# A fused chunked attention and gated MLP on one core: new order entries for the first 430 operations

## The chip, the cores and the metric

One core of a Trainium2 chip. The metric is the device time of one execution in microseconds (us). The kernel before took 373.89 us in the median of 3 runs.

## The reference

Chunked attention over 4 batches, 8 heads and 768 tokens with 8 memory keys, and behind it a gated MLP whose gate is mixed along the tokens:

```python
for c in range(nc):                        # 24 chunks of 32 queries, 16 keys left, 8 right
    k_full = np.concatenate([mem_k, k_ctx], axis=2)
    scores = scale * np.matmul(q_c, k_full.transpose(0, 1, 3, 2))
    a = np.exp(scores - np.max(scores, axis=-1, keepdims=True))
    a = a / (np.sum(a, axis=-1, keepdims=True) + 1e-09)
    out[:, :, c_start:c_end] = np.matmul(a, v_full)
...
h = np.maximum(x @ w_in, 0.0)              # x: 4 x 768 x 512, w_in: 512 x 1024
u, v = (h[..., :d_ff // 2], h[..., d_ff // 2:])
v_n = (v - mu) / np.sqrt(var + 1e-06)
v_s = np.einsum('ts,bsd->btd', w_spatial, v_n) + b_spatial[None, :, None]
return ((u * v_s) @ w_out).astype(np.float32)
```

## The kernel before

The whole kernel is first written down as a list of operations in an object Plan (calls of `op`, numbered 0, 1, 2, ... in the order in which the program makes them) and then laid out by a planner, Plan.order, which runs through the operations with estimated durations, load times and semaphore delays and so makes five fixed lists, one for each of TensorE (PE), ScalarE (ACT), VectorE (DVE), GpSimd (POOL) and SyncE (SP). Each engine works its list strictly in that order and waits at an operation whose inputs aren't there. The planner takes, on each engine, the operation with the smallest sum of possible start and `wait`, and at equal sums the smaller `rank`; of the engines it then advances the one with the earliest pick. An operation that two engines could do stays with the one that would end it first, unless it is pinned. The table ORDER changes this by operation number: it adds to the rank, sets the wait (in us), and pins it to an engine:

```python
if n in ORDER:
    more, wait, only = ORDER[n]
    rank += more
    if only:
        eng = {only: eng[only]}
...
c = (late + ops[n][10], ops[n][4], n)
if pick is None or c < lead:
    pick, lead = (late, ops[n][4], n), c
...
if pick and (best is None or pick < best[0]):
    best = (pick, e)
```

A token tile is 128 tokens, a batch has six (blocks 0 to 5, 6 to 11, ...). For each block `attend` does the keys' rearrangement (`prep`), a burst of 64 small matmuls for the scores, row maximum, subtraction, exponential, row sum and reciprocal (`softmax`), a transposition of the probabilities (`pt`, `pT`), 64 small matmuls with v, the division (`xs`), and a second transposition into x (`xt`, then a high part on ScalarE, line 1122, and a low part on VectorE, line 1126). From block 4 on a burst joins a block's scores and the block before's product with v. Every large product is made of three matmuls (high by high, low by high, high by low), so x and all weights exist as a high and a low part. w_in arrives as 64-bit numbers in eight pieces of 512 KB (four rows of tiles by two halves) and each goes through `from_f64`: a scale (line 1733 or 1735), a shift and a sign step on VectorE (1743, 1749), the high part (597), the rest (1739), an add on GpSimd (1754) and the low part (1761). A v group (`ffn_v`) is 12 matmuls of 512 columns on one block's x with w_in's second half; a u group (`ffn_u`) is 12 matmuls of 384 columns on three blocks' x with a quarter of the first half. Both are line 1172.

The operations that the prediction speaks of, by number. 0, 2, 3: first small loads on ScalarE's queue. 4 to 9: six copies that spread the memory's v rows into the places of blocks 0 to 5 (`first_mem`, line 597). Each place is overwritten in part by that block's v loads, so these loads, on SyncE, wait for the copy. 10, 11 and on: loads, all on SyncE and chained one behind the other in the order of the constant FIRST. 14 to 20 and 22 to 28: the steps of w_in's pieces (1, second half) and (0, second half), 22 being the second one's scale. 56 to 62, 64 to 70, 75 to 81, 83 to 89: the pieces of the first half; 59 and 67 are two high parts, 83 the last piece's scale and 87 its rest step. 97 to 106: shift copies of v for blocks 1 to 5 (line 848). 109 on: blocks 0 to 6; 124 is block 1's exponential (line 1033), 158 block 3's reciprocal, 162 the high part of block 2's x. 207 to 273: the spatial weights, batch 1's v and w_out. 274 on: v and u groups of batch 0, then blocks 7 to 9. The base rank is 10 times the block's number, with 0.5 more for its x, 5 more for its shift copies; for the pieces of w_in it is the fourth field of their entry in FIRST (with 1 more for the rest, the add and the low part); entry 124 has 10, 99 and 100 have 25, 158 has 30.6, 162 has 30.5, 83 has 42.

A load waits until all but 2,000,000 bytes of the loads before it have landed, and for its buffer.

Of the kernel before, what the change touches and what calls it, by code (L numbers as in the profile page):

```python
# [45 lines left out]
    0: (117.6, 6, ''), 1: (1.7, 0, ''), 2: (0, 0.8, ''), 3: (4.8, 0, ''), 5: (20.5, 3, ''),  # L46
    6: (-8.1, 0.4, 'ACT'), 7: (49.4, 6, 'POOL'), 8: (7.1, 0, ''), 9: (-4.8, 0.2, 'ACT'), 10: (48.5, 0.8, ''),
    11: (0, 0.8, ''), 12: (20.6, 0, ''), 13: (-19.7, 0, ''), 14: (36, 0, ''), 15: (26.5, 0.8, ''),
    16: (12.7, 0.4, ''), 17: (16.5, 0, ''), 18: (9, 0.4, ''), 19: (5.9, 0, ''), 20: (10.7, 6, ''),
    21: (24.5, 0.8, ''), 22: (40.1, 3, 'POOL'), 23: (-4.6, 0, ''), 24: (-30.7, 0, ''), 25: (77.8, 0, ''),  # L50
    26: (-164.9, 3, ''), 28: (1.3, 0.8, ''), 29: (-34.6, 1.5, ''), 32: (0, 1.5, ''), 33: (-50.9, 0, ''),
    34: (-67.3, 6, ''), 35: (70.3, 0.2, ''), 36: (-13.8, 0, 'ACT'), 37: (54.9, 0, ''), 39: (21.1, 0, 'ACT'),
    41: (-5.5, 0, ''), 42: (-58.3, 0, 'DVE'), 43: (-7.9, 1.5, ''), 44: (-15.9, 1.5, ''), 45: (-4.8, 0, ''),
    46: (-35.8, 0.8, ''), 47: (0.9, 0, ''), 48: (-53.2, 0, ''), 49: (9.4, 1.5, ''), 50: (-22.6, 0.4, ''),
    51: (-1.6, 0, 'ACT'), 52: (-1.4, 0, ''), 53: (-174.4, 0, ''), 54: (10, 0, 'POOL'), 55: (3.7, 1.5, ''),
# [20 lines left out]
    162: (-45.5, 0, ''), 163: (16.9, 0, ''), 164: (13.1, 0, 'ACT'), 165: (60.6, 0, ''), 166: (-21.3, 0.8, ''),  # L76
# [1824 lines left out]
```

## Time and profile before

| what | value |
|---|---|
| median of 3 runs | 373.89 us (372.83 to 374.18) |
| the profiled execution | 373.35 us, its span 371.6 us |
| TensorE busy | 354.7 us, 95% of the span |
| ScalarE, VectorE, GpSimd busy | 266.4, 246.8, 164.4 us |
| moved | 42.08 MB, 113 GB/s in the mean |
| the chain that ended last | TensorE 89%, DMA 8%, ScalarE 1%, SyncE's queue 1% |

The table is an average over the span. In the page's 40 slices of 9.3 us TensorE is busy by three, seven, six tenths in the first three and by nine or more in all others to the last. The rows below are of the first stages. Times in them are counted from the first instruction; an idle time in brackets stands with the engine or transfer that ended it.

### The profile page before, as it was taken

What the parts mean: (1) busy time and instruction counts of PE and PEld (TensorE: products, weight loads), DVE (VectorE), ACT (ScalarE), POOL (GpSimd) and SP (SyncE); (2) the same over time, 40 slices, a digit from 0 to 9 for tenths busy, and PEclk for the clock granted to TensorE, in tenths of its full rate; (3) what the DMA queues carried; (4) which work ended last, traced back from release to release, by engine and by line L of the source; (5) the groups of instructions that cost most, each with busy time, mean ns of one, the idle gap of its engine ahead of it and who ended that gap; (6) DMA issues with size and microseconds to landing.
All of it is one profiled execution on the core that took longest, in us unless ns stands there. A gap on an engine that the chain in (4) does not pass through costs nothing.

```text
span 371.6 us, 11529 instructions
## 1 busy us (share of the span) xinstructions
PE 354.7 (95%) x4752; PEld 318.4 (86%) x4752; DVE 246.8 (66%) x497; ACT 266.4 (72%) x697; POOL 164.4 (44%) x249
## 2 busy tenths in 40 slices
PE   3769999999999999999999999999999999999996
PEld 3546797999899789899899889899899888999996
DVE  2878878877437375656537267575446798998694
ACT  6686899873585977977876968977966885664262
POOL 4764773573533341442634324424624743224632
PEclk9999999999999999999999999999999999999999
DMA  6989936782024253161024164142130140110004
GB/s 214 287 279 232 344 104 181 232 249 71 25 87 147 93 124 85 35 213 48 17 88 131 62 142 102 49 154 88 37 130 3 57 156 3 43 43 2 0 2 169
DMA packets 30828, 42.08 MB, mean 113 GB/s; under 512 B 5368, under 2 KB 24760, under 8 KB 30776
## 3 DMA queue, kind: packets, MB, share of 16 engines
q1 hardware_dynamic: 30552, 41.27, 36.4%
q8 instruction: 37, 0.61, 0.7%
q14 instruction: 15, 0.12, 0.1%
q10 hardware_dynamic: 224, 0.08, 0.1%
HBM read 35.05 MB, written 6.29 MB: 111 GB/s over the span
## 4 chain that ended last, share of the span: by engine, by line
PE 89%; DMA 8%; ACT 1%; SPq 1%; DVE 0%; issue 0%; ACTq 0%
PE f L1172 69%; PE sx L900 8%; PE f L1399 6%; DMA stage_w<-in_moe_w_in_dram 2%; PE f L1567 2%; DMA big<-in_moe_w_in_dram 2%; DMA q<-in_q_dram 2%; DMA k<-in_k_dram 1%; DMA v<-in_mem_v_dram 1%; SPq L623 1%; PE sx L1567 1%; PE xt L1567 1%; PE pt L1567 1%; PE xt L1116 1%; PE pt L1089 1%; ACT vmain L597 0%
## 5 line engine op out<-in xcount | busy, mean ns | idle before, releaser
L1172 PE MATMUL f<-x,win_h 128*128 128x384 f32 x256 | 72.4, 342 | 0.0
L1172 PE MATMUL f<-win_h,x 128*128 128x512 f32 x192 | 63.4, 411 | 0.5 <-ACT x L1122 0.3
L990 ACT COPY xs<-sx 32x128 f32<-32x128 f32 x240 | 61.6, 257 | 2.9
L1172 PE MATMUL f<-wout,big 128*128 128x512 f32 x216 | 55.7, 394 | 0.0
L1172 PEld LDWEIGHTS f<-x,win_h 128*128 128x128 f32 x256 | 47.0, 188 | 1.4
L1172 PEld LDWEIGHTS f<-wout,big 128*128 128x128 f32 x216 | 39.9, 188 | 7.0 <-DVE big L1671 0.2
L1172 PE MATMUL f<-x,win_l 128*128 128x384 f32 x128 | 43.3, 338 | 0.0
L1172 PEld LDWEIGHTS f<-win_h,x 128*128 128x128 f32 x192 | 35.4, 192 | 8.0 <-DVE x L1126 0.8
L1069 POOL TENSOR_TENSOR p<-p,rec 128x512 f32<-128x512 f32 x15 | 15.7, 1046 | 55.7 <-DVE rec L1046 54.8
L1664 POOL TENSOR_TENSOR st<-st,u 128x384 f32<-128x384 f32 x24 | 25.4, 1060 | 33.0 <-DVE st L1660 17.1
L597 ACT COPY pT<-p 32x128 f32<-32x128 f32 x128 | 37.9, 296 | 2.5 <-POOL p L1069 1.0
L1172 PE MATMUL f<-win_l,x 128*128 128x512 f32 x96 | 38.6, 402 | 0.0
L1218 POOL TENSOR_TENSOR rstd<-ve,mhalf 128x1 f32<-128x1 f32 x24 | 15.9, 663 | 49.5 <-DVE ve L1214 49.3
L597 POOL COPY pT<-p 32x128 f32<-32x128 f32 x112 | 35.5, 317 | 5.1
L1172 PE MATMUL f<-wsp_h,vb 128*128 128x384 f32 x144 | 37.3, 340 | 0.0
L1172 PE MATMUL f<-wsp_h,va 128*128 128x384 f32 x144 | 37.1, 339 | 0.0
L1660 DVE TENSOR_TENSOR st<-f,bias 128x384 f32<-128x384 f32 x24 | 13.4, 556 | 24.8 <-PE f L1172 24.6
L1033 ACT ACTIVATE p<-p 128x512 f32<-128x512 f32 x24 | 15.1, 629 | 19.1 <-DVE p L1018 16.2
L1172 PEld LDWEIGHTS f<-wsp_h,vb 128*128 128x128 f32 x144 | 26.0, 188 | 1.2
L1172 PEld LDWEIGHTS f<-wsp_h,va 128*128 128x128 f32 x144 | 26.0, 188 | 1.1
L900 PEld LDWEIGHTS sx<-k,q 64*32 64x32 f32 x1536 | 17.7, 112 | 9.7 <-issue 4.0
L1039 DVE TENSOR_REDUCE den<-p 128x8 f32<-128x512 f32 x24 | 16.4, 682 | 13.5 <-ACT p L1033 13.4
(225 smaller groups left out, 790.6 us busy)
## 6 DMA issues: line engine op xcount, KB each, us to landing
k<-in_k_dram SPq DMA_DIRECT2D x7, 800.0 KB
q<-in_q_dram SPq DMA_DIRECT2D x7, 768.0 KB
vmain<-in_v_dram SPq DMA_DIRECT2D x38, 128.0 KB
big<-in_moe_w_spatial_dram SPq DMA_DIRECT2D x12, 384.0 KB
out_dram<-st SPq DMA_DIRECT2D x18, 256.0 KB
vmain<-in_v_dram SPq DMA_DIRECT2D x37, 96.0 KB
big<-in_moe_w_in_dram SPq DMA_DIRECT2D x4, 512.0 KB
stage_w<-in_moe_w_in_dram SPq DMA_DIRECT2D x4, 512.0 KB
```

The lines of the kernel that those rows point to most:

```text
L597: return (nc.scalar.copy if e == "ACT" else nc.gpsimd.tensor_copy)(o, a).ins
L900: nc.tensor.matmul(o, w_, m, start=start, stop=True, skip_group_check=True)
L990: last_ = (nc.scalar.copy if e == "ACT" else nc.vector.tensor_copy)(o, a).ins
L1033: nc.scalar.activation(p3, p3, AF.Exp, scale=scale)
L1039: nc.vector.tensor_reduce(d, p3, axis=AX.X, op=ALU.add)
L1069: (nc.vector if e == "DVE" else nc.gpsimd).tensor_tensor(p3, p3, rec, op=ALU.mult)
L1172: return [nc.tensor.matmul(o, ll if x == 1 else lh, rl if x == 2 else rh, start=x == j == 0, stop=j == len(pairs) - 1 and x == (single[-1] ...
L1218: nc.gpsimd.tensor_tensor(a, t_["ve", i], mhalf, op=ALU.pow)
L1399: return [nc.tensor.matmul(o, l_ if x == 1 else h, w_[1] if x == 2 else w_[0], start=first and s == x == 0, stop=s == NQ - 1 and x == 2, s ...
L1567: return [nc.tensor.matmul(o, a[n == 1][:, cols], w2[n == 2], start=first and k == n == 0, stop=k == 1 and n == 2, skip_group_check=True). ...
L1660: nc.vector.tensor_tensor(alloc("st", s_, [P, HT], F32), t_["f", n], bias[:, tok], op=ALU.add)
L1664: nc.gpsimd.tensor_tensor(a, a, t_["u", i], op=ALU.mult)
```

## The change

All entries of ORDER for the operations 0 to 429 are replaced: other amounts added to the ranks (up to some thousands, where before they were up to 271), other waits, and other pins. Entries from 1236 on stay; operations 430 to 1235 have none, before and after. FIRST, the durations and everything else stay, so the loads keep their sequence on SyncE. Of the first 430 operations these lines of the diff hold the entries that the prediction names:

```diff
 ORDER = {
-    0: (117.6, 6, ''), 1: (1.7, 0, ''), 2: (0, 0.8, ''), 3: (4.8, 0, ''), 5: (20.5, 3, ''),
-    6: (-8.1, 0.4, 'ACT'), 7: (49.4, 6, 'POOL'), 8: (7.1, 0, ''), 9: (-4.8, 0.2, 'ACT'), 10: (48.5, 0.8, ''),
...
-    21: (24.5, 0.8, ''), 22: (40.1, 3, 'POOL'), 23: (-4.6, 0, ''), 24: (-30.7, 0, ''), 25: (77.8, 0, ''),
...
-    57: (-25, 0, ''), 58: (-26.3, 0, ''), 59: (7, 0, ''), 60: (-32, 1.5, ''), 61: (-1, 0, ''),
...
-    67: (119.5, 0, 'POOL'), 68: (7.6, 1.5, ''), 69: (-15.6, 0, ''), 70: (-56.9, 0, ''), 72: (-29.9, 6, ''),
...
-    79: (119.2, 0, ''), 80: (14.2, 0, ''), 82: (39.4, 0.8, ''), 83: (-66, 0.2, ''), 84: (32.7, 0.2, ''),
-    85: (17.4, 1.5, ''), 86: (46, 0.2, 'ACT'), 87: (270.8, 0, ''), 88: (64, 0.4, ''), 89: (1.4, 0, ''),
...
-    96: (67.7, 3, ''), 97: (81, 0.4, ''), 98: (68.8, 0.4, ''), 99: (8.7, 0, 'ACT'), 100: (-4.5, 0, 'ACT'),
-    101: (-4.9, 3, ''), 102: (23.5, 0.4, 'ACT'), 103: (-19.2, 0.2, 'ACT'), 104: (30.4, 3, 'POOL'),
-    105: (3.3, 6, 'ACT'), 106: (93, 6, 'POOL'), 107: (28.8, 0, ''), 108: (-3.3, 0.8, 'POOL'),
...
-    124: (-14.6, 0.4, ''), 126: (19.9, 0.8, ''), 127: (-29.2, 0, ''), 128: (0.2, 0, ''), 129: (-2.6, 0, ''),
...
-    156: (-6.2, 0.2, ''), 157: (107.6, 0, ''), 158: (-31.9, 0.4, ''), 160: (-32.3, 0, ''), 161: (-3, 0, ''),
-    162: (-45.5, 0, ''), 163: (16.9, 0, ''), 164: (13.1, 0, 'ACT'), 165: (60.6, 0, ''), 166: (-21.3, 0.8, ''),
...
+    0: (-26.9, 0, ''), 1: (-8.1, 0, ''), 2: (-6.4, 0, ''), 3: (-46.2, 0, ''), 4: (112.9, 0, ''),
+    5: (-99.3, 0, ''), 6: (-278.2, 1.5, 'POOL'), 7: (-200.9, 0.2, 'POOL'), 8: (-41.7, 0.8, 'POOL'),
+    9: (-891.5, 3, 'POOL'), 10: (-61.1, 6, ''), 11: (125.5, 0.8, ''), 13: (38.5, 0, ''), 14: (-133.5, 0, ''),
...
+    19: (-265.4, 0.4, ''), 20: (-1084.6, 0.2, ''), 21: (36.5, 0, ''), 22: (-46.3, 0, 'ACT'), 23: (5.2, 0, ''),
...
+    56: (949.7, 0.2, 'ACT'), 57: (429.8, 0, ''), 58: (619.7, 0.8, ''), 59: (292.2, 0, 'POOL'),
...
+    64: (-105.9, 0, 'ACT'), 65: (-77.3, 0, ''), 66: (1401.2, 0, ''), 67: (175.1, 0, 'ACT'),
...
+    83: (-787.5, 0, 'ACT'), 84: (132.2, 0, ''), 85: (-837.3, 0.4, ''), 86: (-202.1, 0, ''), 87: (-122, 0, ''),
...
+    98: (-37.7, 0, ''), 99: (64.2, 0.8, ''), 100: (113.1, 0, ''), 101: (-2301.8, 1.5, 'ACT'),
+    102: (25.5, 0, ''), 103: (-235, 0.2, 'ACT'), 104: (-48.3, 1.5, ''), 105: (901.8, 0, ''),
+    106: (-489.1, 3, ''), 107: (-42.8, 0, ''), 108: (-8.2, 0, 'POOL'), 109: (84, 0.2, ''), 110: (510.7, 0, ''),
...
+    122: (-239.8, 0, ''), 123: (-2.4, 0, ''), 124: (211.8, 0, ''), 125: (-138.8, 0, ''),
...
+    154: (120.1, 0, ''), 155: (345.2, 0, ''), 156: (-16.1, 0, ''), 157: (-71.4, 0, ''), 158: (-1239.3, 1.5, ''),
+    159: (-1009.4, 0, ''), 160: (-247.6, 0, ''), 161: (-54.7, 0, ''), 162: (-325.5, 0, ''),
...
```

Pins that differ from where the operation ran before: 6 and 9 go from ACT to POOL, 22 from POOL to ACT, 59 from ACT to POOL, 67 and 101 from POOL to ACT. Others are set or lifted where that alone moves nothing: of the shift copies 97 to 106, for example, 99, 100, 102, 104, 105 and 106 lose their pin.

## Rows read from the trace of the kernel before

**Rows 1.** Stretches: length, busy time and instructions of each engine, clock, DMA.
```profile
0.00:16.00 16.00, 7.34 (x215) 5.97 (x221) 7.55 (x19) 9.94 (x16) 9.04 (x16) 1.00 0.77 253
16.00:31.00 15.00, 11.33 (x253) 8.15 (x243) 12.27 (x22) 11.78 (x22) 8.41 (x9) 1.00 0.93 270
31.00:38.57 7.57, 6.50 (x107) 4.37 (x89) 5.44 (x9) 5.60 (x12) 5.40 (x7) 1.00 0.88 206
38.57:80.00 41.43, 41.43 (x829) 37.04 (x830) 34.61 (x74) 37.07 (x68) 24.32 (x22) 1.00 0.71 215
80.00:300.00 220.00, 219.95 (x2981) 198.01 (x2980) 129.57 (x249) 165.51 (x489) 91.82 (x175) 1.00 0.30 93
```
**Rows 2.** Chain that ended last, in time: start, length, what.
```profile
...
5.31 1.05 ACT vmain L597
...
6.38 0.34 SPq L623
...
27.01 9.06 DMA stage_w<-in_moe_w_in_dram
```
**Rows 3.** TensorE's timeline: start, length, line, operation, count, idle before.
```profile
...
20.88 1.11 PE L1089 MATMUL pt<-ident,p 128*128 128x128 f32 x4 [1.42 <-ACT p L1033]
...
26.57 1.12 PE L1089 MATMUL pt<-ident,p 128*128 128x128 f32 x4 [1.80 <-ACT p L1033]
...
28.34 0.63 PE L1172 MATMUL f<-win_l,x 128*128 128x512 f32 x1
...
31.67 0.39 PE L1172 MATMUL f<-win_l,x 128*128 128x512 f32 x1
...
37.84 0.50 PE L1172 MATMUL f<-win_h,x 128*128 128x512 f32 x1 [0.28 <-ACT x L1122]
38.57 0.50 PE L1172 MATMUL f<-win_h,x 128*128 128x512 f32 x1 [0.23 <-DVE x L1126]
...
53.06 0.34 PE L1172 MATMUL f<-x,win_h 128*128 128x384 f32 x1
53.24 0.63 PE L1172 MATMUL f<-win_h,x 128*128 128x512 f32 x2
```
**Rows 4.** ScalarE's timeline.
```profile
...
19.34 0.83 ACT L848 COPY vmain<-vmain 24x768 f32<-24x768 f32 x1 [0.21 <-DMA vmain<-in_v_dram]
20.20 0.63 ACT L1033 ACTIVATE p<-p 128x512 f32<-128x512 f32 x1
...
36.09 0.67 ACT L1739 ACTIVATE stage_w<-stage_w 128x512 uint32<-128x512 uint32 x1 [1.07 <-DMA stage_w<-in_moe_w_in_dram]
```
**Rows 5.** VectorE's timeline.
```profile
...
10.50 0.81 DVE L1743 TENSOR_SCALAR st<-st 128x512 uint32<-128x512 uint32 x1
...
12.07 0.38 DVE L1743 TENSOR_SCALAR st<-st 128x512 uint32<-128x512 uint32 x1
...
17.37 0.69 DVE L1018 TENSOR_TENSOR p<-sx,mx 128x512 f32<-128x512 f32 x1
...
20.86 0.69 DVE L1039 TENSOR_REDUCE den<-p 128x8 f32<-128x512 f32 x1 [2.46 <-ACT p L1033]
...
52.15 0.68 DVE L1126 TENSOR_TENSOR x<-xt,x 128x512 fp32r<-128x512 f32 x1
```
**Rows 6.** GpSimd's timeline.
```profile
...
5.38 1.04 POOL L597 COPY v<-v 128x1024 f32<-128x1024 f32 x1
...
8.74 1.52 POOL L1735 TENSOR_SCALAR st<-big 128x512 f32<-128x512 f32 x1 [1.33 <-DMA big<-in_moe_w_in_dram]
10.21 0.83 POOL L597 COPY v<-v 128x768 f32<-128x768 f32 x1
12.78 2.78 POOL L1754 TENSOR_TENSOR st<-st,big 128x512 uint32<-128x512 uint32 x2 [1.74 <-ACT win_h L597]
```
**Rows 7.** TensorE groups by shape, 38.57 to 53.24: count, busy, mean ns, idle.
```profile
L1172 PE MATMUL f<-x,win_h 128*128 128x384 f32 x30 | 8.5, 343 | 0.0
L1172 PE MATMUL f<-x,win_l 128*128 128x384 f32 x15 | 5.1, 339 | 0.0
```

More of the change, by code (lines that the diff above doesn't have):

```diff
@@ L51 @@
[L51 to L55, printed above, removed]
@@ L56 @@
-    57: (-25, 0, ''), 58: (-26.3, 0, ''), 59: (7, 0, ''), 60: (-32, 1.5, ''), 61: (-1, 0, ''),
-    62: (79.9, 0, 'POOL'), 63: (89, 0, ''), 64: (-9.9, 0, ''), 65: (-49.8, 0, ''), 66: (29, 0, ''),
-    67: (119.5, 0, 'POOL'), 68: (7.6, 1.5, ''), 69: (-15.6, 0, ''), 70: (-56.9, 0, ''), 72: (-29.9, 6, ''),
-    73: (18.4, 1.5, ''), 75: (87.5, 0, ''), 76: (15.8, 0.4, ''), 77: (-5.7, 0.2, ''), 78: (-51.4, 0, ''),
-    79: (119.2, 0, ''), 80: (14.2, 0, ''), 82: (39.4, 0.8, ''), 83: (-66, 0.2, ''), 84: (32.7, 0.2, ''),
@@ L76 @@
-    162: (-45.5, 0, ''), 163: (16.9, 0, ''), 164: (13.1, 0, 'ACT'), 165: (60.6, 0, ''), 166: (-21.3, 0.8, ''),
[12 rows of a table removed]
-    239: (35.7, 0, ''), 241: (23.6, 0, ''), 242: (-1.8, 0.8, ''), 243: (-46.7, 0, 'ACT'), 244: (-141.6, 0, ''),
-    245: (-14.5, 0, ''), 246: (-59, 0, 'ACT'), 247: (21.4, 0, ''), 248: (17.7, 0, ''), 249: (0.5, 0, ''),
-    250: (9.5, 1.5, ''), 252: (-5.1, 0, ''), 253: (8.9, 0, ''), 255: (-0.6, 0.4, ''), 257: (109.2, 0.4, 'DVE'),
-    258: (10.3, 0, ''), 259: (-58.8, 0, ''), 260: (3, 0, ''), 261: (45.9, 0, ''), 262: (-14.7, 0, 'ACT'),
@@ L93 @@
-    263: (-93.6, 0, ''), 264: (-14.6, 0, ''), 265: (-47.7, 0, ''), 266: (-31.5, 0, ''),
-    267: (-72.1, 1.5, 'ACT'), 268: (165, 0, ''), 269: (-0.7, 0, ''), 271: (-16.9, 0, ''), 273: (9, 0, ''),
[27 rows of a table removed]
+    0: (-26.9, 0, ''), 1: (-8.1, 0, ''), 2: (-6.4, 0, ''), 3: (-46.2, 0, ''), 4: (112.9, 0, ''),
+    5: (-99.3, 0, ''), 6: (-278.2, 1.5, 'POOL'), 7: (-200.9, 0.2, 'POOL'), 8: (-41.7, 0.8, 'POOL'),
+    9: (-891.5, 3, 'POOL'), 10: (-61.1, 6, ''), 11: (125.5, 0.8, ''), 13: (38.5, 0, ''), 14: (-133.5, 0, ''),
@@ new lines @@
+    15: (-1182.7, 0.8, ''), 16: (95.1, 0.2, ''), 17: (39.7, 0.2, ''), 18: (-154.9, 0, ''),
+    19: (-265.4, 0.4, ''), 20: (-1084.6, 0.2, ''), 21: (36.5, 0, ''), 22: (-46.3, 0, 'ACT'), 23: (5.2, 0, ''),
+    24: (52.3, 0, ''), 25: (-4.7, 0, 'ACT'), 26: (606.7, 0.4, ''), 27: (103, 6, ''), 28: (-13.8, 0, ''),
+    29: (-361.6, 0, ''), 30: (-42, 0, ''), 32: (185.6, 6, ''), 33: (1.7, 0, ''), 34: (-255.2, 0, ''),
+    35: (30.8, 0.8, ''), 36: (12.1, 0, 'ACT'), 37: (28.5, 0, ''), 38: (28.2, 0, ''), 39: (-69.1, 0, 'ACT'),
[3 rows of a table added]
@@ new lines @@
+    56: (949.7, 0.2, 'ACT'), 57: (429.8, 0, ''), 58: (619.7, 0.8, ''), 59: (292.2, 0, 'POOL'),
+    60: (594.6, 0.8, ''), 61: (270.7, 0, ''), 62: (-1174.4, 0, 'POOL'), 63: (53.4, 1.5, ''),
+    64: (-105.9, 0, 'ACT'), 65: (-77.3, 0, ''), 66: (1401.2, 0, ''), 67: (175.1, 0, 'ACT'),
+    68: (-661.1, 0.8, ''), 69: (29.5, 0, ''), 70: (29.3, 0, 'DVE'), 71: (49.3, 0, ''), 72: (-182, 0, ''),
+    73: (95.5, 0.2, ''), 74: (189.6, 0, ''), 75: (1191.3, 0, 'ACT'), 76: (217.9, 0, ''), 77: (64.6, 0, ''),
+    78: (188.9, 0.2, ''), 79: (527.7, 0, ''), 80: (-16, 0, ''), 81: (-91.7, 0, ''), 82: (130.1, 0.2, ''),
@@ new lines @@
+    83: (-787.5, 0, 'ACT'), 84: (132.2, 0, ''), 85: (-837.3, 0.4, ''), 86: (-202.1, 0, ''), 87: (-122, 0, ''),
+    88: (-560, 3, ''), 89: (-1018.4, 0, ''), 90: (-494.3, 0, ''), 91: (-340.4, 0.2, ''), 92: (-93.5, 0, ''),
+    93: (6.2, 6, ''), 94: (170.9, 0, ''), 95: (99.2, 0, ''), 96: (-1617.4, 6, ''), 97: (33.6, 0, ''),
+    98: (-37.7, 0, ''), 99: (64.2, 0.8, ''), 100: (113.1, 0, ''), 101: (-2301.8, 1.5, 'ACT'),
+    102: (25.5, 0, ''), 103: (-235, 0.2, 'ACT'), 104: (-48.3, 1.5, ''), 105: (901.8, 0, ''),
@@ new lines @@
+    106: (-489.1, 3, ''), 107: (-42.8, 0, ''), 108: (-8.2, 0, 'POOL'), 109: (84, 0.2, ''), 110: (510.7, 0, ''),
+    111: (217.1, 0, ''), 112: (-0.8, 0, ''), 114: (-124.4, 0, ''), 115: (124.6, 0, ''), 116: (30.1, 0, ''),
+    117: (131.9, 0, ''), 118: (72.8, 0.4, 'ACT'), 119: (103.7, 0, ''), 120: (450.3, 6, ''), 121: (-83.9, 0, ''),
+    122: (-239.8, 0, ''), 123: (-2.4, 0, ''), 124: (211.8, 0, ''), 125: (-138.8, 0, ''),
+    126: (-2098.5, 0.4, ''), 127: (-264.1, 0, ''), 128: (-451.2, 0, ''), 129: (-584.3, 0.2, ''),
@@ L122 @@
+    130: (-177.3, 0, ''), 131: (-257.6, 0, ''), 132: (634.5, 0.2, ''), 133: (577, 0.2, 'ACT'),
[26 rows of a table added]
+    264: (271.6, 0, ''), 265: (-2.2, 0, ''), 266: (299.7, 0.8, ''), 267: (195.2, 0.4, 'ACT'),
[33 rows of a table added]
     1242: (79.2, 1.5, ''), 1244: (34.4, 0, ''), 1245: (228.1, 0, 'ACT'), 1246: (404.9, 0, ''),
```

3 lines of the change are left out of this document (removed), and 107 rows, old and new, of the table ORDER.

## The prediction

> **What bounds the kernel now.** I read the stretches first [rows 1]. From 38.57 us on TensorE has no gap worth the name: busy 41.43 of 41.43 and 219.95 of 220 us. Before 38.57 it stands still for 16 - 7.34 = 8.66 us, then 15 - 11.33 = 3.67 us, then 7.57 - 6.50 = 1.07 us. So the span is the moment at which TensorE becomes saturated plus 333.0 us of work that the change doesn't reduce; only a part of 13.4 us is to be had.
>
> Then the chain that ended last [rows 2]: up to 38.57 us it is mostly loads, not TensorE. ScalarE's copy into vmain at 5.31 us releases SyncE at 6.38; SyncE's queue is in order, so the loads of v, of q and k for blocks 1 and 2 and of more w_in go out behind it; by way of these the last w_in quarter is in flight from 27.01 to 27.01 + 9.06 = 36.07. ScalarE has that quarter's first step queued at 36.09 and runs it before block 2's x, and TensorE's run without gaps starts at 38.57 [rows 3].
>
> Third, TensorE's own lines before saturation [rows 3]. Its waits after 16 us were on the exponentials of block 1 (1.42 us before the transposes at 20.88) and of block 2 (1.80 us before 26.57). Here the pace matters as well: one 128x512 matmul took 0.63 us at 28.34 and 0.39 us at 31.67, although the granted clock in [rows 1] is 1.00 throughout. TensorE had run without a gap from 26.57 on before the faster pace showed.
>
> Last, who held whom. ScalarE [rows 4]: block 1's differences were ready at 17.37 + 0.69 = 18.06 us [rows 5], its exponential began at 20.20, because a shift copy of 0.83 us, which itself waited for a DMA, stood just ahead of it. VectorE [rows 5]: it sat 2.46 us until that exponential, with a sign step of w_in ready behind it in its list. Such hold-ups in a fixed list are what another order can change.
>
> **The change part by part.** The instructions, their shapes and the load sequence stay. Entries for operations 0 to 429 get new ranks, waits and pins; counted through the program they reach from the start to block 9's exponential.
>
> The pins that move work for certain are few. The copies of operations 6 and 9 go from ScalarE to GpSimd (1.04 us for one [rows 6]), the scale of operation 22 from GpSimd to ScalarE (1.52 us there [rows 6], about 0.67 on ScalarE, as its pass over a tile of that size at 36.09 [rows 4]), 59 and 67 trade places, and the shift copy 101 goes from GpSimd to ScalarE (a copy's 1.04 again). ScalarE: -2.1 + 0.67 + 1.04 = -0.4 us; GpSimd: +2.1 - 1.52 - 1.04 = -0.5 us. Neither is a bound before 38 us, so I cost the moves themselves at nothing; their cover is GpSimd's idle time between its copies and its first add at 12.78 us [rows 6]. If that cover were gone, the add of w_in would come later by a copy, 1.04 us.
>
> Two more copies on GpSimd run beside VectorE. What the rows show of such company: a shift of VectorE took 0.81 us at 10.50, beside a GpSimd copy that ran from 10.21, and the next one 0.38 us at 12.07, when GpSimd stood idle [rows 5, 6]. So a copy in the wrong place costs VectorE 0.43 us, two 0.86, and what they delay is the first v group, which stands in front of TensorE's gap of 1.42 us and is covered by it: nought in the sum. The Trainium skill (SBUF — State Buffer, Who interferes with whom) speaks against this move: it calls the port pair that both engines share an exclusive lock, on which the later instruction waits for the whole of the earlier one. By that rule two copies could cost VectorE 2.1 us, an estimate, of which 1.42 fill the gap and 0.7 come through; the sum below would lose the 0.7 it has for that gap and 0.7 more and come out at 374.4. The trace agrees in kind, but with 0.43 us, not a whole copy; the row decides.
>
> Operation 4, the copy that releases SyncE, loses its first place: its rank goes from 0 to 112.9, and operation 5, which either engine may run, now ranks at 10 - 99.3 = -89.3. If ScalarE takes 5 first and GpSimd takes 4 right after the key copy, it starts at 5.38 as GpSimd's first copy does now [rows 6], against 5.31: 0.07 us. If it waits behind 5 on ScalarE, all loads behind it are late by 1.05 us [rows 2]. GpSimd is free and the planner compares both engines' ends, so I take 0.1 us and keep 1.05 for the range. Queued behind that load on SyncE are the v, q and k loads of blocks 0 to 2 and then all of w_in.
>
> The hold-ups. Block 1's exponential (124) gets rank 10 + 211.8 = 221.8, the shift copies 99 and 100 rank 25 + 64.2 = 89.2 and 25 + 113.1 = 138.1, and all four early shift copies lose or lack a pin. So its rank does not put the exponential ahead of the copies; it comes first only where they have gone to GpSimd or were not ready. Of the 1.42 us between nothing and all comes back. Block 2's 1.80 us needs its scores sooner, and those follow block 1's. The 0.23 us before 38.57 and what ScalarE lost waiting 1.07 us for the last w_in quarter [rows 4] could come back if block 2's x goes ahead of that step: its rank is 30.5 - 325.5 = -295, the step's (87) 43 - 122 = -79, but the scale's behind it (83) 42 - 787.5 = -745.5. Before, x ranked ahead too (-15 against 313.8) and still ran after: what put it there was readiness in the plan and a load that landed late, not rank.
>
> Upper bound on the gain: all of TensorE's idle after 16 us, 3.67 + 1.07 = 4.7 us; the 8.66 us before wait on the first loads, which keep their sequence. Bound below: a loss of 1.05 us by operation 4, more in the slow rival. What follows saturation also caps the gain. In the 14.67 us from 38.57 to 53.24 TensorE ran 45 of the 48 matmuls of the first four u groups [rows 7]; at 53.24 - 53.06 = 0.18 us from start to start only 3 x 0.18 = 0.5 us of these was left when the next v group began at 53.24 [rows 3], and its last input, block 3's low part, had ended at 52.15 + 0.68 = 52.83 [rows 5]. So a TensorE that is ahead by more than about 1 us finds nothing to do there unless blocks 3 to 5 come sooner too, and these go through ScalarE, busy 37.07 of the 41.43 us from 38.57 to 80 [rows 1].
>
> Sum: from 0 to 1.42 + 0.28 + 0.23 = 1.9 us by the two hold-ups with a releaser that another order can move (0.28 and 0.23 stand before TensorE's matmuls at 37.84 and 38.57 [rows 3]); I take the middle, 0.71 + 0.25 = 0.95 us, since the ranks promise neither, less 0.1 for operation 4: 0.85 us. The profiled execution took 373.35 us, 1.75 above its span, and would take 372.5. The median of the runs, 373.89, lies 0.54 higher: 373.0 us.
>
> **The rivals.** First, the new order closes the gaps as a whole. Then the 1.42 and most of the 1.80 us go, and the faster pace comes a few us sooner: at 0.39 instead of 0.63 us for a matmul the 5.1 us from 26.57 to 31.67 [rows 3] would shrink by up to 5.1 x 0.24 / 0.63 = 1.9. The Trainium skill's clock gate (TensorE: Matmul & The Clock Gate, Part 1) says the throttled state is the default and sustained activity releases it. The trace agrees: 0.63 us fell to 0.39 after steady work. Together at most 1.42 + 1.80 + 1.9 = 5.1 us; with what the inputs after 53 us leave of it I put it at 2 to 4.5, so 369.4 to 371.9, middle 370.6. For it: the hold-ups are plain in the rows. Against: x of blocks 3 to 5 must all move with it. Chance 0.28.
>
> Second, slower: block 3's x comes later. Its place is 53.24 us, where TensorE's ready work is 0.5 us. Up to 0.5 + (53.24 - 52.83) = 0.9 us of lateness is free; beyond that each microsecond is a microsecond of span. Block 3's way there goes through ScalarE and VectorE lists that are over 80% busy (VectorE 34.61 of 41.43 us [rows 1]), and its reciprocal (158) gets a wait of 1.5, where it had 0.4. A block that is 2 to 4 us late costs 1.1 to 3.1: 375.0 to 377.0, middle 376.0. For it: the list is as tight there as a list can be, and operation 4 behind a copy would add to it (374.9 alone, not measurable). Against: ScalarE has 41.43 - 37.07 = 4.4 us left there in which to catch up. Chance 0.24, of which 0.18 lies above 375.8.
>
> Third, the change does next to nothing: the loads land when they land, [rows 2] is a chain of loads until 36.07, and the new lists meet the same waits. Then 373.9, within 0.3. Chance 0.12.
>
> **How the numbers follow.** Forecast, a gain between 0 and 1.9 us, 0.36; nothing, 0.12; first rival 0.28; second 0.24. A measurement of this kernel tells about 0.5%, 1.87 us, from no change: same is 372.0 to 375.8. Faster is the first rival, 0.28; same is forecast, third and the lower end of the second, 0.36 + 0.12 + 0.06 = 0.54; slower 0.18. From 370.0 to 376.0 the range leaves out about 0.07 of the first rival and 0.12 of the second; the forecast's own range is 372.0 to 374.9, its upper end operation 4 behind a copy.
>
> **What would show it.** Right: TensorE's last wait in the new trace lies between 36.5 and 38.6 us and none of size follows; the two waits on exponentials, 1.42 + 1.80 us [rows 3], fall by about 1 together; SyncE's first long wait still ends near 6.4. The first rival shows as a 128x512 matmul at 0.39 us before 29 us. The second shows as a wait on x between 50 and 60 us, where now there is none. Operation 4 shows as SyncE's issue at 7.4 instead of 6.38. I am wrong if saturation moves by over 2 us, or if TensorE gets waits after 80 us, where the rest of the plan's lists may be laid out anew though their entries are unchanged.

## The result, and the profile after

The changed kernel took 377.44 us (median; 374.59 to 380.48), the kernel before, measured beside it, 372.81 us: a ratio of 1.0103, interval 1.0064 to 1.0142. The change makes the kernel slower by about 1%, outside the predicted range of 370.0 to 376.0 and on the other side of the forecast.

The execution that was profiled is the longest of its ten: 380.48 us, span 378.7. It is a slow run, over 1.5% above the shortest, so nothing that it alone shows is taken for the cause. Because single times differ so much, two more executions of the same program were profiled later (spans 375.0 and 374.5); where a reading holds for all three I say so.

The same stretches as in [rows 1], for TensorE alone: start and end, length, busy time and instructions, granted clock, share of the DMA engines, GB/s.

```profile
0.00:16.00 16.00, 6.52 (x172) 1.00 0.80 250
16.00:31.00 15.00, 9.68 (x251) 1.00 0.97 289
31.00:38.57 7.57, 4.39 (x135) 0.97 0.81 201
38.57:80.00 41.43, 39.37 (x797) 0.92 0.59 176
80.00:300.00 220.00, 219.59 (x2929) 1.00 0.31 93
```

The third and fourth lines carry most of the loss. From 31 to 38.57 us TensorE was busy for 4.39 us, before it was 6.50; from 38.57 to 80, where it used to be busy without a gap, it stands still for 41.43 - 39.37 = 2.06 us, and the clock is 0.92 in the mean. The last line has a small one: 0.41 us idle instead of 0.05.

TensorE's timeline shows where: start, length, operation, count, and in brackets the idle time before it and what ended it.

```profile
20.52 1.12 PE L1101 MATMUL pt<-ident,p 128*128 128x128 f32 x4 [3.19 <-ACT p L1045]
...
24.75 0.40 PE L1184 MATMUL f<-win_l,x 128*128 128x512 f32 x1
...
26.26 0.66 PE L1101 MATMUL pt<-ident,p 128*128 128x128 f32 x4 [0.33 <-ACT p L1045]
...
29.42 0.66 PE L1128 MATMUL xt<-ident,xs 128*128 128x128 f32 x4 [1.80 <-DVE xs L982]
...
33.82 0.40 PE L1184 MATMUL f<-win_l,x 128*128 128x512 f32 x1
37.40 0.66 PE L1101 MATMUL pt<-ident,p 128*128 128x128 f32 x4 [3.18 <-ACT p L1045]
...
39.37 0.63 PE L1184 MATMUL f<-win_l,x 128*128 128x512 f32 x1
...
60.55 0.80 PE L912 MATMUL sx<-k,q 64*32 64x64 f32 x60
...
61.21 0.59 PE L912 MATMUL sx<-v,pT 64*32 64x64 f32 x37
63.85 0.43 PE L912 MATMUL sx<-v,pT 64*32 64x64 f32 x25 [2.06 <-issue]
...
65.64 1.05 PE L1128 MATMUL xt<-ident,xs 128*128 128x128 f32 x4
...
218.84 0.73 PE L1184 MATMUL f<-win_h,x 128*128 128x512 f32 x2 [0.28 <-ACT st L1709]
```

The kernel before, at block 3's transposes, in a line that [rows 3] leave out:

```profile
35.08 0.66 PE L1089 MATMUL pt<-ident,p 128*128 128x128 f32 x4 [0.57 <-ACT p L1033]
```

Read it against [rows 3]. Block 1's wait on its exponential did not shrink but grew, from 1.42 to 3.19 us; block 2's fell from 1.80 to 0.33, and 1.80 us of waiting appeared before block 2's second transposition. The faster pace (0.40 us for a 128x512 matmul) is there at 24.75 us, 7 us earlier than the row of before at 31.67. Then come three things that the kernel before did not have, or not in this size: 3.18 us before block 3's transposes (0.57 before), a stop of 2.06 us in the middle of block 6's burst, behind 103 of its 128 matmuls and with no engine that ended it, and a wait of 0.28 us at 218.84.

After each of the two long gaps the clock falls to half for a while, as the same view of narrower stretches shows:

```profile
38.13:41.54 3.41, 3.41 (x12) 0.50 0.95 328
41.54:65.43 23.89, 21.83 (x478) 1.00 0.50 145
65.43:68.85 3.42, 3.42 (x12) 0.50 0.79 197
```

TensorE is busy throughout these 3.4 us, but at half the pace (0.63 us at 39.37, where it had 0.40 at 33.82), so each of them costs up to 3.41 / 2 = 1.7 us of work.

Why block 3's transposes waited is on ScalarE's timeline:

```profile
35.62 0.66 ACT L1745 ACTIVATE stage_z<-stage_w 128x512 f32<-128x512 f32 x1 [3.45 <-DMA stage_w<-in_moe_w_in_dram]
36.19 0.65 ACT L1751 ACTIVATE stage_w<-stage_w 128x512 uint32<-128x512 uint32 x1
36.73 0.61 ACT L1045 ACTIVATE p<-p 128x512 f32<-128x512 f32 x1
37.25 0.67 ACT L1751 ACTIVATE stage_w<-stage_w 128x512 uint32<-128x512 uint32 x1
```

On VectorE's, block 3's differences:

```profile
32.33 0.69 DVE L1030 TENSOR_TENSOR p<-sx,mx 128x512 f32<-128x512 f32 x1
```

And in the chain that ended last, in time (start, length, what), as in [rows 2]:

```profile
26.23 9.37 DMA stage_w<-in_moe_w_in_dram
...
61.80 2.06 issue
```

The differences were ready at 32.33 + 0.69 = 33.02 us. Its exponential (155) started at 36.73, because ScalarE's new list has two steps of the last w_in piece to arrive, its scale (83) and its rest (87), ahead of it, and that piece was in flight from 26.23 to 35.60; in [rows 2] it landed at 36.07, but there nothing that TensorE needed stood behind it but block 2's x. In the list before, the order was 75, 79, 155, 87, 83, 162: the last piece's steps stood behind block 3's exponential, and those of the piece before it, which arrives sooner, ahead. The new order is 83, 87, 155, 79, 75, 162. The texts below call these the six operations; 155 and 162 keep their places in the six, and the four steps around 155 are turned round.

The account of the three executions goes by three marks on TensorE: the start of block 6's burst, the start of block 7's, and the end. The new list has three more matmuls of a v group ahead of block 6's burst, which the stretch behind it then lacks (0.65 us: where nothing stops it takes 7.29 us instead of 7.94). All in us; each stretch's difference from the kernel before in brackets:

| execution | start of block 6's burst | from there to block 7's burst | from there to the end | span |
|---|---|---|---|---|
| before | 57.01 | 7.94 | 306.6 | 371.6 |
| after | 60.55 (+3.5) | 11.04 (+3.1) | 307.1 (+0.5) | 378.7 |
| after, second (376.81) | 56.54 (-0.5) | 11.35 (+3.4) | 307.1 (+0.5) | 375.0 |
| after, third (376.34) | 56.29 (-0.7) | 11.12 (+3.2) | 307.1 (+0.4) | 374.5 |

So in the two executions near the median the change had made a gain up to block 6's burst: 0.5 to 0.7 us, and 0.65 us of work more done, 1.1 to 1.4 us in all. All of it and 2 to 3 us more went in the 8 us behind that mark. Only the profiled, longest one had lost its time before.

### The profile page after: what moved, and what is told of

Same layout as the page of the kernel before. It is cut to its first block, busy times and chain, and to the rows that moved or that the text cites. A ratio compares the mean times of both kernels' runs of the same rounds, so it can differ in the third digit from the quotient of the medians.

```text
span 378.7 us, 11529 instructions
## 1 busy us (share of the span) xinstructions
PE 354.9 (94%) x4752; PEld 319.3 (84%) x4752; DVE 245.8 (65%) x498; ACT 267.6 (71%) x701; POOL 160.1 (42%) x244
## 4 chain that ended last, share of the span: by engine, by line
PE 77%; ACT 9%; DMA 9%; DVE 2%; issue 2%; SPq 0%; ACTq 0%
PE f L1184 58%; PE sx L912 7%; PE f L1411 6%; ACT xs L1002 4%; DMA big<-in_moe_w_in_dram 4%; ACT pT L609 3%; DMA stage_w<-in_moe_w_in_dram 2%; PE f L1579 2%; DMA q<-in_q_dram 1%; DMA k<-in_k_dram 1%; PE xt L1128 1%; ACT p L1045 1%; PE sx L1579 1%; PE xt L1579 1%; PE pt L1579 1%
## 5 line engine op out<-in xcount | busy, mean ns | idle before, releaser
L1184 PE MATMUL f<-win_h,x 128*128 128x512 f32 x192 | 64.5, 418 | 0.4 <-ACT st L1709 0.3
L1184 PEld LDWEIGHTS f<-win_h,x 128*128 128x128 f32 x192 | 36.4, 199 | 7.4 <-ACT st L1709 1.3
L609 ACT COPY pT<-p 32x128 f32<-32x128 f32 x132 | 39.1, 296 | 4.0 <-POOL p L1081 2.3
```

What stands on the lines that cost most here:

```text
L609: return (nc.scalar.copy if e == "ACT" else nc.gpsimd.tensor_copy)(o, a).ins
L1184: return [nc.tensor.matmul(o, ll if x == 1 else lh, rl if x == 2 else rh, start=x == j == 0, stop=j == len(pairs) - 1 and x == (single[-1] ...
```

## What the experiments were to tell apart

Two theories at the start. T1: ScalarE's new order of the last two w_in pieces around block 3's exponential (six operations) is the cause. T2: the stop inside block 6's burst is the cause, and it comes from the delivery of TensorE's own instructions. The trace has a transfer queue of kind "instruction" whose every transfer is 16 KB; there are 37 on TensorE's queue in each execution, for 9,557 recorded TensorE instructions: one for about 256. A burst joined with the product before it takes 256 instructions in some 1.4 us. The kernel's planner reckons with this too (its class Pages has a page of 256 instructions), which I had not weighed in the prediction.

All edits move entries in an engine's list behind the planner, with a helper `put(n, m, behind)` that takes operation n out and puts it ahead of m (0) or right behind it (1); or they change the number of idle matmuls at the start (PADS, four TensorE instructions each).

### The changed kernel again

> The changed kernel as it is, for a second profile. Theory 1 (ScalarE's list has the steps of the last w_in piece ahead of block 3's exponential, and TensorE stands still until that piece has landed): a TensorE wait of about 3 us before block 3's transposes near 34 to 37 us in this profile too. Theory 2 (an instruction fetch of TensorE is late inside block 6's burst): a stop of about 2 us near 62 us without a releaser. Theory 3 (what the profile shows at these two places is chance of that one execution, and the loss lies elsewhere): at least one of the two is missing while the time stays near 377. Single times spread from 374.6 to 380.5.

377.09 us (376.61 to 378.04), ratio 1.0093, interval 1.0067 to 1.0119. The profiled execution is the second of the table. It had no wait of 3 us before block 3's transposes, since the last w_in piece came earlier (ScalarE ran its scale at 32.40), but the stop in block 6's burst was there, 2.39 us, and half clock from 61.18 to 64.59 behind it. So the loss does not need the 3.18 us.

### ScalarE's six operations put back, and put into the kernel before

```diff
 order = self.order()          # changed kernel: b_undo
+put(75, 83, 0)
+put(79, 83, 0)
+put(87, 155, 1)
+put(83, 87, 1)
 
 order = self.order()          # kernel before: c_fault
+put(83, 75, 0)
+put(87, 75, 0)
+put(79, 155, 1)
+put(75, 79, 1)
```

> The changed kernel with six operations of ScalarE's list put back in the order of the kernel before: scale and rest of w_in piece (2, first half), block 3's exponential, rest and scale of piece (3, first half). Everything else as changed. Theory 1: the wait of 3.2 us before block 3's transposes falls to about 1 us or less, no stretch at half the clock near 38 to 41 us, and the median falls by 1.5 to 3 us to 374.5 to 376. Theory 2 alone: no change, near 377.4. Theory 3: no change.

374.96 us (373.85 to 375.61), ratio 1.0031, interval 1.0013 to 1.0049. More than half of the loss goes: 2.1 us against the changed kernel beside it (377.09). The ten times lie within 1.8 us, those of the changed kernel within 5.9; but the same program's later times (p_undo) lie within 4.2, so that the scatter goes too is not shown. The stop in block 6's burst is still there with 1.68 us, but the clock stayed at full behind it.

> The kernel before with that same stretch of ScalarE's list in the order of the changed one: scale and rest of piece (3, first half), block 3's exponential, rest and scale of piece (2, first half). Theory 1: TensorE waits 2 to 4 us more before block 3's transposes, the median rises by 1.5 to 3 us to 374.3 to 376, and single runs spread as in the changed kernel. Theories 2 and 3: as before, 372.8.

373.78 us (372.69 to 377.45), ratio 1.0024, interval 0.9995 to 1.0053. In the kernel before, the same six operations in the wrong order cost little: in the profiled execution (373.05) ScalarE ran block 3's exponential at 35.09 instead of 34.41, TensorE's transposes came at 35.77 without a wait, and nothing stopped later. TensorE of this execution reached that point no sooner than the exponential; with the new lists it was there at 34.2 and 33.5 us in two of three executions, and waited. The time lies between the two theories' ranges and its interval holds 1.000, so that the order costs anything by itself in the kernel before is not shown.

### Is it where the bursts lie in the instruction pages?

```diff
-    for _ in range(PADS):
+    for _ in range(PADS + 12):     # d_pads: changed kernel; f_undo_p12: six operations put back
+    for _ in range(PADS + 5):      # e_undo_p5: six operations put back
+    for _ in range(PADS - 6):      # g_before_m6: kernel before; h_before_both: with c_fault's edit
```

> The changed kernel with 30 instead of 18 of the tiny matmuls at its start (they end before the first scores can begin), so that every later instruction of TensorE lies 24 places further on in the program, and fetches of its instructions fall elsewhere; the lists of all engines stay. Theory 2: the stop of 2 us near 62 us is gone or smaller and the median falls by 2 to 3.5 us, to 374 to 375.5, unless another fetch falls badly. Theory 1 alone: near 377.4 with the wait near 34 to 37 us.

376.5 us (373.78 to 379.28), ratio 1.0084, interval 1.0051 to 1.0117. The stop left block 6's burst, and one of 0.91 us appeared in block 5's. In this execution block 3's transposes waited 2.52 us. (Twelve idle matmuls are 48 instructions, where the expectation has 24 places.) The time is between the two ranges: by itself it decides nothing.

> The changed kernel with ScalarE's six operations in the order of the kernel before (as in the run b_undo) and 5 more of the tiny matmuls at the start, 20 instructions on TensorE. If both theories hold (the order of the w_in steps, and a fetch of instructions that falls due just ahead of block 6's burst), the stop inside that burst is gone or under 0.5 us and the median falls from 375.0 to 373.0 to 373.8, level with the kernel before. If the stop in the burst costs nothing in the end, 375.0.

375.36 us (373.55 to 377.22), ratio 1.0056, interval 1.0026 to 1.0087: not the 373.0 to 373.8 expected. The stop had moved to just behind block 5's burst (1.32 us).

> The same with 12 more tiny matmuls (48 instructions), as in the run d_pads, where the stop went from block 6's burst (2.1 us) to block 5's (0.9 us). Both theories: 373.5 to 374.5. Without the second: 375.0.

375.82 us (374.06 to 378.01), ratio 1.0068, interval 1.0030 to 1.0105, with 1.46 us in block 5's burst: above the range of either theory. A second stop without a releaser, 0.63 us at 133.12, lies behind the 4289th instruction, nine times 256 behind the 1985th.

> The kernel before with 6 fewer tiny matmuls at the start, 24 instructions on TensorE, so that the same fetch falls due just ahead of block 6's burst, as in the changed kernel. Second theory: a stop of 1.5 to 2.5 us without a releaser inside that burst (57 to 61 us), and a median 1 to 2.5 us above the kernel before: 374.3 to 375.8. If not: as before, 373.3, or a little less for the shorter start.

374.02 us (372.23 to 377.17), ratio 1.0007, interval 0.9978 to 1.0037. The profiled execution is its longest: a stop of 2.28 us in block 6's burst, and half clock from 61.36 behind it, in the kernel before with nothing changed but that six idle matmuls are left out. The median is below the 374.3 to 375.8 expected and its interval holds 1.000: the stop can come without the change, but a cost of this shift in the median is not shown.

> The kernel before with both faults put in: ScalarE's six operations as in the changed kernel and 6 fewer tiny matmuls. If these two are the loss, 375.5 to 377.5, with single runs spread over 4 us or more as in the changed kernel; if the loss lies elsewhere in the new lists, under 375.

375.06 us (372.48 to 378.73), ratio 1.0044, interval 1.0006 to 1.0082; the profiled execution is its shortest, with a stop of 0.18 us. The median lies between the two expected ranges, at the edge of the lower, and decides nothing.

What follows. Counting TensorE's instructions from the start, every stop in block 6's burst, in every kernel, lies behind the 1985th, and each of those in block 5's in these runs behind the 1729th: exactly 256 apart, whatever the shift. So the stop belongs to an address in the instruction stream. But to shift the bursts against it cures nothing, because with two bursts of a page each one of them always crosses an edge.

### What decides whether it stops

Fourteen of the profiled executions side by side, in the order of the last column but one: when block 6's burst began, when the page behind the 1985th instruction had been fetched, and the stop.

| kernel | burst starts | page landed | landed after the start | stop, us |
|---|---|---|---|---|
| before | 57.01 | 55.19 | -1.82 | 0 |
| c_fault | 56.71 | 55.33 | -1.38 | 0 |
| m_after_wsp | 57.08 | 56.32 | -0.76 | 0 |
| q_undo_wsp | 57.59 | 57.28 | -0.31 | 0 |
| h_before_both | 55.71 | 55.83 | 0.12 | 0.18 |
| k_undo_wsp | 56.29 | 56.77 | 0.48 | 0.59 |
| p_undo | 56.57 | 57.07 | 0.50 | 0.87 |
| o_undo_wsp | 56.77 | 57.45 | 0.68 | 0.86 |
| b_undo | 56.78 | 57.64 | 0.86 | 1.68 |
| i_undo_loads | 57.13 | 58.27 | 1.14 | 1.40 |
| after | 60.55 | 62.30 | 1.75 | 2.06 |
| after, third | 56.29 | 58.08 | 1.79 | 2.12 |
| after, second | 56.54 | 58.57 | 2.03 | 2.39 |
| g_before_m6 | 56.86 | 59.09 | 2.23 | 2.28 |

The later the page lands after the burst's start, the longer the stop, with three pairs of neighbours out of order by up to 0.3 us. In the six other profiled executions it landed at least 1.8 us ahead of the burst, and none stopped there. In nine of the ten that stop TensorE goes on 1.4 to 1.6 us after the page has landed, in b_undo 2.1 us after. So the late page is what stops TensorE. From the 1729th instruction, 256 ahead of the edge, to the start of this fetch it took 1.1 to 2.4 us on the old lists (six executions), 5.0 to 5.1 us in all three executions of the changed kernel, and 3.6 to 3.9 us in the five with ScalarE's six operations put back and the bursts and loads left alone; but 3.0 us in m_after_wsp, where the six stand wrong. What makes the fetch late was the next question.

### Small loads, or TensorE's own order?

w_sp stands for the spatial weights: six pieces, each with a high part made on ScalarE and a low part on GpSimd. The reciprocal root of tile 0 is a step of that token tile's normalization, which GpSimd does.

```diff
 # on top of b_undo's edit
+for n in range(225, 233):      # i_undo_loads: eight small loads ahead of w_sp's piece 1
+    put(n, 219, 0)

+put(325, 194, 0)               # j_undo_two: two steps of u and v ahead of block 6's burst
+put(339, 194, 0)

+put(208, 211, 0)               # k_undo_wsp: w_sp's high parts in the old order
+put(280, 212, 1)

 # kernel before
+put(330, 194, 0)               # l_before_swap: both bursts one step later
+put(175, 179, 0)
```

> The new lists with ScalarE's six operations back in the old order, and SyncE's eight small loads of mem_v (24 KB each) put ahead of the load of w_sp's piece 1, so that they are over some 4 us before TensorE reaches block 6's burst. Theory that these loads hold up the fetch of TensorE's next 256 instructions: the fetch starts within about 2 us of the 1728th instruction (3.9 us without the edit), the stop of 1.9 us in block 6's burst goes, 373.0 to 373.8 us. Theory that the fetch waits for something in TensorE's own order: stop and time stay, 374.6 to 375.4. The loads could also take buffers too early for other loads; then the time rises with no stop in the burst.

373.83 us (372.49 to 375.39), ratio 1.0023, interval 1.0002 to 1.0044. The loads were out by 48.2 us, 9 us ahead of the burst, yet in the profiled execution the fetch started 4.85 us behind the 1729th instruction and the burst stopped for 1.40 us. These eight loads are not what holds the fetch up. The median is lower than b_undo's, but the intervals overlap.

> The new lists with ScalarE's six operations back, and two groups of u (12 matmuls, about 1.2 us of TensorE) put ahead of block 6's burst. If the loss that is left (374.96 against 373.2) is the stop in the burst, for which 256 instructions come too late, the 1.2 us of work ahead of it gives the fetch time: the stop falls from 1.9 to 0.7 us or to nothing, 373.2 to 374.2 us. If the loss lies elsewhere, and the stop only takes time that would be lost later, the time stays at 374.6 to 375.4 though the stop is smaller.

375.19 us (373.4 to 376.95), ratio 1.0043, interval 1.0008 to 1.0078. What the edit moved are two steps of three matmuls each, one of u and one of v (12 instructions, 1.2 us), not twelve matmuls. The fetch was early in this execution (53.32, or 0.84 us behind the 1729th instruction) and the burst's own stop gone, but the time is not better: behind the burst TensorE waits 0.78 us for VectorE (at 60.83) and 0.94 us for ScalarE (at 71.60), and the clock was at half from 31.1 to 34.5. Work put ahead of one burst is not a cure either.

> The new lists with ScalarE's six operations back, and the high part of w_sp's piece 3 ahead of that of piece 4 on ScalarE (in the new lists GpSimd, which takes piece 3 first, waits for the second of the two), with the reciprocal root of tile 0 behind piece 4's low part on GpSimd as before the change. SyncE reaches w_sp's next load and the small loads about 1.3 us sooner. Theory of the loads: the fetch comes sooner by as much, the stop of 1.9 us falls to about 0.6 us, 373.5 to 374.2 us. Theory of TensorE's own order: 374.6 to 375.4.

373.68 us (372.17 to 379.39), ratio 1.0022, interval 0.9989 to 1.0055; the stop was 0.59 us. It looked as if the order of w_sp's parts, by which SyncE waits longer for GpSimd, were the second cause.

> The kernel before with two swaps of the change on TensorE alone: block 5's burst behind block 3's transposes of x, and block 6's burst behind one more group of tile 7. If TensorE's own order brings the late fetch, a stop of 1.5 to 2 us comes into block 6's burst or right behind block 5's, 374.2 to 375.0 us. If the loads bring it, nothing changes: 372.8 to 373.6.

373.08 us (372.73 to 374.11), ratio 1.0009, interval 0.9992 to 1.0026. These two swaps of TensorE's order cost nothing by themselves in the kernel before.

### w_sp's part: a second cause?

```diff
 # changed kernel: m_after_wsp
+put(208, 211, 0)
+put(280, 212, 1)

 # kernel before, with c_fault's edit: n_before_all
+put(208, 211, 1)
+put(209, 208, 1)
+put(280, 212, 0)
```

o_undo_wsp and q_undo_wsp are k_undo_wsp's program, p_undo is b_undo's and r_after the changed kernel's.

> The changed kernel with the w_sp part alone put back (piece 3's high part ahead of piece 4's on ScalarE, tile 0's reciprocal root behind piece 4's low part on GpSimd); ScalarE's six operations stay in the new order. Theory of two causes that add: 377.1 less 1.2 makes 375.5 to 376.3 us, with the wait of some 3 us at block 3's exponential still there in a run that has it and a shorter stop, or none, in block 6's burst. Theory that the six operations are the whole of it: 376.8 to 377.6 us.

375.73 us (372.46 to 378.12), ratio 1.0068, interval 1.0036 to 1.0101. The profiled execution (373.26) is far below the median: 1.11 us of waiting at block 3's transposes, no stop and no half clock.

> The kernel before with both parts of the change put in: ScalarE's six operations in the new order, and on ScalarE piece 4's high part ahead of piece 3's, with tile 0's reciprocal root ahead of piece 4's low part on GpSimd. Theory that these two are causes in themselves: 373.0 + 0.8 + 1.2, so 374.6 to 375.4 us, with a stop in block 5's or 6's burst. Theory that they cost only on the new lists, whose TensorE runs ahead of them: 373.0 to 374.0 us.

375.28 us (373.1 to 377.9), ratio 1.0061, interval 1.0036 to 1.0086. The time came as two causes have it, the sign did not: in the profiled execution (374.01) nothing stops in block 5's or 6's burst; TensorE waits 0.76 us for an exponential at 70.11 instead, and 0.6 us more for ScalarE and VectorE up to 78.

> The new lists with both parts put back, a second time, for the interval: if the two parts are the whole loss, 372.7 to 373.6 us; if 0.7 us is left in the rest of the new lists, 373.5 to 374.0 us and an interval that lies above 1.000.

373.35 us (371.66 to 376.14), ratio 1.0003, interval 0.9978 to 1.0028. Up to here the times of all three spoke for two causes that add. (They ran side by side, so m_after_wsp less this one, 375.73 - 373.35 = 2.4 us, is a second measure of ScalarE's six operations, with w_sp's part put back in both.) So the last three kernels ran side by side:

> The new lists with ScalarE's six operations back, a second time and beside the next kernel, which differs from it by w_sp's part alone. If w_sp's part is a cause of its own: 374.6 to 375.2 us, 1.2 to 1.7 above the next kernel, with a stop of 1.5 to 2 us in block 5's or 6's burst. If it is not: both kernels at 373.4 to 374.4 us.

373.85 us (372.1 to 376.34), ratio 1.0024, interval 1.0000 to 1.0047.

> The new lists with both parts back, a third time. If the two parts are the whole loss: 372.9 to 373.7 us, an interval that holds 1.000, and a stop in the bursts of 5 and 6 of under 1.1 us. If the rest of the new lists costs something too: 374 us or more.

373.82 us (371.8 to 375.29), ratio 1.0015, interval 0.9992 to 1.0038.

> The changed kernel on the same chip as the two above: 376.5 to 377.6 us if the two parts add to 3.5 to 4 us, and 1.8 to 2.5 us above the kernel with ScalarE's six operations back.

376.39 us (373.74 to 381.41), ratio 1.0092, interval 1.0065 to 1.0119.

The kernels with and without w_sp's part differ by 0.03 us. The second cause, at 1.2 to 1.7 us, falls: side by side nothing of it is seen, though intervals of 1.8 us leave room for some tenths, and the earlier differences (1.3 us between b_undo and k_undo_wsp, which ran apart) were about as large as the scatter between two runs of one program (b_undo 374.96, p_undo 373.85). That w_sp's part matters only while ScalarE's six operations stand wrong, as m_after_wsp and n_before_all would have it, is possible and not shown.

What stands: ScalarE's six operations are 376.39 - 373.85 = 2.5 of the 3.4 us; the two other pairs that ran side by side gave 2.1 and 2.4. TensorE's lines show where the time goes, in one execution of each kernel. First the third execution of the changed kernel, at block 3's transposes, block 6's burst and behind it, and its stretch from 60.19 to 63.60 us (columns as above):

```profile
34.65 0.66 PE L1101 MATMUL pt<-ident,p 128*128 128x128 f32 x4 [1.12 <-ACT p L1045]
...
56.29 0.80 PE L912 MATMUL sx<-k,q 64*32 64x64 f32 x60
...
59.66 0.43 PE L912 MATMUL sx<-v,pT 64*32 64x64 f32 x25 [2.12 <-issue]
...
61.87 0.63 PE L1184 MATMUL f<-win_l,x 128*128 128x512 f32 x1
```

```profile
60.19:63.60 3.41, 3.41 (x12) 0.50 0.90 230
```

Then p_undo, with the six operations back:

```profile
33.37 0.64 PE L1109 MATMUL pt<-ident,p 128*128 128x128 f32 x4
...
56.57 0.80 PE L920 MATMUL sx<-k,q 64*32 64x64 f32 x60
...
58.69 0.43 PE L920 MATMUL sx<-v,pT 64*32 64x64 f32 x25 [0.87 <-issue]
```

```profile
60.19:63.60 3.41, 3.41 (x20) 1.00 0.65 171
```

Where nothing stops, the stretch from block 6's burst to block 7's is 7.29 us on the new lists (q_undo_wsp, m_after_wsp). The third execution's 11.12 are 7.29 + 2.12 of stop + 1.71 of half clock. p_undo's 8.30 are 7.29 + 0.87, and 0.14 that I can't place. Between these two executions, then, the 1.12 us at block 3's transposes were made up for by block 6's burst, which begins 0.28 us sooner in the changed kernel; what tells them apart at the end is 1.25 us of stop and 1.71 us of clock.

The rest of about 0.8 us (p_undo, interval from nought to 1.8): at least 0.4 us of it is in every profiled execution of the new lists, behind block 7's burst (307.1 us or more against 306.6), as waits of 0.28 us at 218.84 (above) and 0.13 at 133.5 where the kernel before has none.

## Why the prediction was wrong

**The bound.** Right as far as it went: the span is the moment of saturation plus work that the change doesn't reduce. But I treated the work behind 38.57 us as a constant, because TensorE had no gap there. It was gapless with a cover of 1.82 us (the page landed that much ahead of block 6's burst), and no row of [rows 1 to 7] looked at the instruction fetches. This is the step that failed most: 3.1 to 3.4 us of every profiled execution of the changed kernel lie in the stretch that I took as fixed.

**The hold-ups.** The gain of 0 to 1.9 us, 0.85 taken, is about what the marks show up to block 6's burst in two of three executions: 1.1 to 1.4 us. The sign that I had named failed: block 1's wait grew to 3.19, 3.25 and 2.82 us in the three executions, and block 1's and 2's waits together did not fall by 1 but rose from 3.22 to between 3.5 and 3.8 us. That is no later exponential. Block 1's started at 19.84, 19.09 and 18.36 us instead of 20.20, and its transposes came 0.4 to 1.8 us sooner. But of the six matmuls of a v group that stood in front of these transposes (16.53 to 19.46 us; transposes at 20.88) TensorE's new list has none there: the first three come behind them (transposes at 20.52). The first of the six, before and after:

```profile
16.53 1.22 PE L1172 MATMUL f<-win_h,x 128*128 128x512 f32 x2
```

```profile
21.29 1.20 PE L1184 MATMUL f<-win_h,x 128*128 128x512 f32 x2
```

I had this v group standing in front of the gap and looked at no new order of TensorE's own, so a wait by itself was a poor sign of a hold-up. The rows also have the faster pace, at 23 to 25 us instead of after 28.34; which of the two makes the gain was not tested. The sum also left out a third wait on an exponential, block 3's 0.57 us at 35.08, though the 1.07 us of idle time that it took from [rows 1] hold it: 0.57 + 0.28 + 0.23.

**Operation 83.** I saw that its new rank of -745.5 goes ahead of block 2's x, asked only whether the 0.23 us there and ScalarE's 1.07 come back, and put no loss down for it. The operation that mattered stood in the same stretch of the list: block 3's exponential, 155, whose rank goes up by 345.2 - 12.7 = 332.5 in the same table. I held the rank of the step against one operation, not against all of its stretch. That is the failed step of the sum: it put the move of the last piece's steps ahead of block 3's exponential at nothing, and put back, the six operations give 2.1 to 2.5 us.

**The rivals.** The first rival's marker came true (0.40 us at 24.75, before 29 us) and its price of 2 to 4.5 us did not: the cap that I gave, what the inputs after 53 us leave, was not even what held it. The second rival had the sign and nearly the time (375 to 377), but the wrong place: no wait on x lies between 50 and 60 us. Operation 4 was no matter: it stayed ScalarE's first copy, and SyncE's issue behind it stands at 6.18 us where [rows 2] have 6.38 (SyncE's timeline of the changed kernel):

```profile
6.18 1.68 SPq L635 DMA_DIRECT2D vmain<-in_v_dram  x4
```

The copies on GpSimd I had right at nought, but one reading of theirs was off: of the copy that ran from 10.21 [rows 6] only 10.21 + 0.83 - 10.50 = 0.54 us were left when VectorE's shift started, so its 0.43 us more are most of that rest, and the row doesn't speak against a wait for the end of the copy.

**What I had said would show me wrong** did: waits after 80 us (0.41 us idle in the last line of the stretches instead of 0.05). Saturation came sooner, in two of three executions by over 2 us: the last wait before the long run ended at 37.40, 30.46 and 34.65 us in the three, where the kernel before has 38.57, and the time followed none of them.

**Open.** Why the fetch starts 5.0 to 5.1 us behind the 1729th instruction in the changed kernel and 3.6 to 3.9 us with six ScalarE operations of 20 us earlier put back: that these operations cost the time is shown, by what path they delay the page is not. The eight small loads are excluded, and the two swaps of the bursts in the kernel before. That TensorE's own order matters is not excluded: in j_undo_two, with six matmuls moved ahead of the burst, the fetch came after 0.84 us. Loads as a whole were not tried; the planner's class Pages lets a fetch wait until the loads sent before it are through, but the share of the DMA engines alone doesn't sort the cases: from the 1729th instruction to the fetch it is 0.82 in the kernel before, and 0.57 to 0.63 in the three executions of the changed one. How far TensorE's queue of instructions runs ahead of the engine was not tried either.

## What to carry to other kernels

An order that a plan finds better can still put a step that waits for the last load ahead of a step that TensorE needs: compare each moved rank with everything in its stretch of the list, and look for the operation whose input comes last. A gain upstream is only kept if the saturated stretch behind it has cover everywhere, and bursts of hundreds of tiny instructions are where it has least. Where single times of one program scatter by 1 to 2%, two kernels 1 us apart are only told apart side by side.

## What the hardware showed that I had not expected

TensorE's instructions are brought by transfers of 16 KB while the kernel runs, 37 of them here, each for about 256 instructions, taking 0.9 to 2.0 us. The Trainium skill (Trainium Architecture — The Big Picture, The software stack) has the streams moved into each engine's instruction memory when a program is loaded. No run here shows the loading; the trace shows that it isn't all, with 37 transfers within the span. A page that lands 1.75 us after a burst's start stops TensorE for 2.06 us. The queue's line, in the view of transfers of the changed kernel from 60.5 to 62.5 us (packets, MB, share of 16 engines):

```profile
q8 instruction: 1, 0.02, 4.7%
```

And a stop is not paid once: those of 2.06, 2.12, 2.28 and 2.39 us in block 6's burst were each followed by a stretch at a granted clock of 0.50 that cost up to 1.7 us more, those of 0.87, 1.40 and 1.68 us by none. The mean granted clock of the changed kernel's ten single times goes with them: 1.00 for the three from 374.59 to 375.46 us, 0.995 for those from 376.44 to 377.88, 0.99 for those from 378.61 to 380.48. Across kernels the mean clock tells nothing of the kind: c_fault's profiled execution has 0.986, with half clock from 23.41 to 33.65 us, where TensorE still had waits, and took 373.05 us.
